# Transposing attention weights with the DMA crossbar instead of the matrix engine

## The chip, the cores and the metric

The kernel runs on one core of a Trainium2 chip. A core has five engines that run their own instruction queues in order: TensorE (PE, matrix multiplications, with a separate row for its weight loads, PEld), VectorE (DVE), ScalarE (ACT), GpSimd (POOL) and SyncE (SP), which here issues all DMAs. Engines meet only through semaphores. PE writes to PSUM, the others work mostly in SBUF, 128 partitions wide. The metric is the device time of one execution in microseconds, the median of the runs; lower is better.

## The reference

Attention that keeps the 32 largest scores of each row, and then a feed-forward block with a hard-swish gate.

```python
B, H, S, D = 8, 8, 576, 64          # float32 throughout
scores = (1 / sqrt(D)) * q @ k.T
kth    = 32nd largest of each row
scores = where(scores >= kth, scores, -1e9)
attn   = exp(scores - max) / (sum + 1e-9)
x      = (attn @ v)                 # (B,H,S,D) -> (B*S, H*D) = (4608, 512)
h      = x @ w_in                   # (512, 2048)
out    = (h * clip(h + 3, 0, 6) / 6) @ w_out   # (2048, 512)
```

## The kernel before

Work is cut into 80 *duos* (L184). A duo is two head pairs (a `Pair`, L138, is two heads of one batch element, put one above the other on the 128 partitions) and one tile of query rows. S = 576 is four tiles of 128 rows and a rest of 64; a full duo has two rows of 576 scores per partition and head pair (`nt = 2`), a duo of the rests has one (`nt = 1`), because both heads' 64 rows share the partitions. A batch element has ten duos, eight full ones and two of rests, in the order full, full, rest, full, full, full, full, rest, full, full.

The order of all instructions is written by hand (`tc.manual_schedule()`, L66) in the loop over steps `m` (L482). What a step issues on each engine stands in that engine's queue in just that order. In step `m`:

- DVE does the eight rounds `top(0)` to `top(7)` of duo `m` (L240): four for head pair u=0, four for u=1. A round finds the next 8 largest values of each row (MAX8, L247) and, but for the last round, strikes them out (MATCH_REPLACE8, L251).
- `prev.exp(1)` and, after `top(3)`, `u.exp(0)` (L256): POOL computes the negated threshold `kth` (L262) and `shift` (L263, L264) from the scan, ACT applies a very steep Prelu (L267) and Exp (L272), which also sums the row into `den`; POOL adds a small constant to it (L277).
- `duos[m+1].scores()` (L197): PE multiplies q and k for the next duo into `big`, the one five-bank PSUM tile, and ACT copies the scores to `sc` (L230, L233; three buffers).
- after `top(1)`, `prev.weights()` (L279): one reciprocal of `den` on DVE (L281) for both head pairs, then four scalings of a row each on POOL (L285).
- after `top(2)`, `prev.transpose()` (L289): 18 PE transposes of 128x128 blocks (12 for rests) from `sc` into `big` (L298), and one ACT copy of all of them to `eT` (L302).
- after `top(6)`, `values(m - 1)` (L418, L304): PE multiplies v by `eT` (L316), ACT copies the result into `xT`, the input of the feed-forward (L323). When a tile of 256 rows is complete, its feed-forward block is put into the list `todo`.
- `piece(n)` (L394) takes the next pieces of the feed-forward generator (L327) from that list: PE's `h` (L340), ACT's relu (L348), DVE's gate (L352, issued two pieces later), PE's `acc` (L361), ACT's scaling and SP's store of the output (L371, L373). How many pieces a step takes depends on the length of the list when the program is built. What is left after the last step follows at the end.

In the first steps every round also calls `convert_step`. The weights `w_in` and `w_out` come as 64-bit floats and are turned into 32-bit ones in 32 chunks (`convert`, L97): SP loads a chunk `st` (L103), ACT takes both halves of each word apart (L108, L111), POOL clamps (L109), and one or two conversion steps later DVE shifts and combines (L117, L118) and POOL adds (L122).

The loads of the next batch element's k and q (`load`, L145, six DMAs) and v (`load_values`, L159, four DMAs) are issued by SP after `top(0)` in the fourth to seventh step of a batch, one pair a step; its k and q are transposed by PE (L176) after `top(4)` of the sixth to ninth step. v lies in a ring of eight sets of tiles, `vm` and `vr`, and k's rests in `kr`. The pool `kq` has nine buffers of 4.6 KB per partition, which hold `landed`, the transposed `kq` and the chunks `st`. SP takes its DMAs strictly in the order of the program, and each waits there for what it needs.

Of the kernel before, what the change touches and what calls it, by code (L numbers as in the profile page):

```python
# [9 lines left out]
ALU = mybir.AluOpType  # L10
F32 = mybir.dt.float32
U32 = mybir.dt.uint32
I32 = mybir.dt.int32
PSUM = bass.MemoryType.PSUM

TOP_K = 32
# [11 lines left out]
def kernel(  # L28
# [22 lines left out]
    def pool(name, bufs, **kw):  # L51
        return ctx.enter_context(tc.tile_pool(name=name, bufs=bufs, **kw))

    consts = pool("consts", 1)
    kqpool = pool("kq", 2 * NHP + 1)
    scpool = pool("sc", 3)
    wkpool = pool("wk", 1)
    mpool = pool("m", 4)
    etpool = pool("et", 1)
    xtpool = pool("xt", 2)  # L60
    xrpool = pool("xr", 1)
    gpool = pool("g", 8)
# [14 lines left out]

    ring = []  # L80
    for i in range(2 * NHP):
        vm = const([P, 2, J, D], f"vm{i}")
        vr = const([P, 2, D], f"vr{i}")
        kr = const([P, 2, R], f"kr{i}")
        nc.gpsimd.memset(vr[:], 0.0)
        nc.gpsimd.memset(kr[:], 0.0)
        ring.append((vm, vr, kr))

    def big():

        return ps_big.tile([P, 5 * 512], F32, tag="big", name="big")
# [46 lines left out]
    class Pair:  # L138


        def __init__(self, b, hp):
            self.b, self.hp = b, hp
            self.vm, self.vr, self.kr = ring[(b * NHP + hp) % len(ring)]

        def load(self):  # L145
            h0 = 2 * self.hp
# [23 lines left out]
        def transpose(self):  # L170
            kq = kqpool.tile([P, JP + S], F32, tag="kq", name="kq")
            self.kT, self.qT = kq[:, 0:JP], kq[:, JP : JP + S]
            ps = big()
            for j in range(2 * J + 1):
                rows = self.landed[:, j, :, :].rearrange("p h d -> p (h d)")
                nc.tensor.transpose(ps[:, j * P : (j + 1) * P], rows, ident[:])  # L176
            c0 = 2 * JP
            nc.scalar.copy(kq[:, 0:c0], ps[:, 0:c0])
            nc.scalar.copy(kq[:, c0 : c0 + R], ps[:, c0 + R : c0 + 2 * R])
            for hh in range(2):  # L180
                d = slice(hh * D, (hh + 1) * D)
                nc.scalar.copy(self.kr[d, hh, :], ps[d, c0 : c0 + R])  # L182

    class Duo:  # L184
# [6 lines left out]
        def __init__(self, pairs, qt):  # L191
            self.pairs, self.qt = pairs, qt
            self.rest = qt == J
            self.nt = 1 if self.rest else 2
            self.nb = J + 2 if self.rest else 2 * J + 1

        def scores(self, us=(0, 1)):  # L197

# [41 lines left out]
        def top(self, u, r):  # L240

            if r == 0:
                self.m = mpool.tile([P, 2, TOP_K], F32, tag="m", name="m")
                self.wk = wkpool.tile([P, 2, S], F32, tag="wk", name="wk")
                self.cur = [self.row(u, t) for t in range(self.nt)]
            for t in range(self.nt):
                nc.vector.max(self.m[:, t, 8 * r : 8 * r + 8], self.cur[t])  # L247
# [28 lines left out]
            d = self.den[:, u, 0:nt]  # L276
            nc.gpsimd.tensor_scalar_add(d, d, EPS)  # L277

        def weights(self):  # L279
            d = self.den[:, :, 0 : self.nt]  # L280
            nc.vector.reciprocal(d, d)  # L281
            for u in range(2):
                for t in range(self.nt):
                    row = self.row(u, t)
                    nc.gpsimd.tensor_scalar(  # L285
                        row, row, self.den[:, u, t : t + 1], 1.0, ALU.mult, ALU.mult
                    )

        def transpose(self):  # L289

            starts = [c * P for c in range(J)]
            starts += [JP, S - P] if self.rest else [c * P for c in range(J, 2 * J + 1)]
            eT = self.eT = etpool.tile([P, 2 * (2 * J + 1), P], F32, tag="eT", name="eT")
            ps = big()
            n = 0
            for u in range(2):
                for c0 in starts:
                    nc.tensor.transpose(  # L298
                        ps[:, n * P : (n + 1) * P], self.sc[:, u, c0 : c0 + P], ident[:]
                    )  # L300
                    n += 1
            nc.scalar.copy(eT[:, 0:n, :].rearrange("p c q -> p (c q)"), ps[:, 0 : n * P])  # L302

        def values(self, dst):  # L304

            w = R if self.rest else P
            pv = ps_w.tile([P, 512], F32, tag="w", name="pv")
            for u in range(2):
                pr, eT = self.pairs[u], self.eT[:, u * self.nb : (u + 1) * self.nb, :]
                for c in range(J + 1):  # L310
                    for hh in range(2):
                        if self.rest:
                            rhs = eT[:, c if c < J else J + hh, hh * R : (hh + 1) * R]
                        else:
                            rhs = eT[:, c if hh == 0 or c == J else J + 1 + c, :]
                        nc.tensor.matmul(  # L316
                            pv[hh * D : (hh + 1) * D, u * w : (u + 1) * w],
                            pr.vm[:, hh, c, :] if c < J else pr.vr[:, hh, :],
                            rhs,
                            start=(c == 0),  # L320
                            stop=(c == J),
                        )
            nc.scalar.copy(dst, pv[:, 0 : 2 * w].rearrange("p (u q) -> p u q", u=2))  # L323
# [56 lines left out]
    duos = []  # L380
    for b in range(B):
        halves = [pairs[b][0:2], pairs[b][2:4]]
# [5 lines left out]
    per_batch = 2 * J + 2  # L388
    ND = len(duos)
# [4 lines left out]
    def piece(count=1):  # L394
        nonlocal left
        for _ in range(count):
            while todo:
                try:
                    gates.append(next(todo[0]))
                    left -= 1  # L400
                    break
                except StopIteration:
                    todo.pop(0)
            else:
                gates.append(None)
            if len(gates) > 2:
                gate = gates.pop(0)
                if gate:
                    gate()
# [69 lines left out]
    convert_step(2)  # L479
    first[3].load()  # L480

    for m in range(ND + 1):  # L482
        u = duos[m] if m < ND else None
        prev = duos[m - 1] if m else None


        level = (left >= 10) + (left >= 20)
        if u and u.rest:
            count = [(1, 0, 1, 0), (1, 0, 1, 1), (1, 1, 1, 1)][level]
        else:  # L490
            count = [(2, 1, 2, 1), (2, 2, 2, 1), (2, 2, 2, 2)][level]
        depth = 2 if m < 2 else 1

        def top(r):
            if u:
                u.top(r // 4, r % 4)
            convert_step(depth)

        if m:
            prev.exp(1)  # L500
        else:
            first[2].transpose()
            first[3].transpose()
        if m + 1 < ND:
            duos[m + 1].scores()
        top(0)
        piece(count[0])
        p = pair_at(m, 3)
        if p:
            p.load()  # L510
            p.load_values()
        if m == 0:
            first[0].load_values()
# [22 lines left out]
        if m:  # L536
            values(m - 1)
        top(7)
        if m == 2:
            piece(3)  # L540
    while todo:
        piece()
    piece(2)


# [1 line left out]
_INS = ["q", "k", "v", "moe_w_in", "moe_w_out"]  # L547
# [30 lines left out]
```

## Time and profile before

| | |
|---|---|
| median of 3 runs | 1737.13 us (1736.5 to 1737.71) |
| the profiled execution | 1738.36 us |
| its span, first to last instruction | 1736.6 us |
| mean granted TensorE clock | 0.967 |
| PE busy | 1607.3 us, 93% of the span |
| DVE busy | 1544.7 us, 89% |
| ACT busy | 947.1 us, 55% |
| POOL busy | 413.8 us, 24% |
| DMA queue of SP | 100,992 packets, 54.55 MB, 11.4% of 16 engines |

Busy time is the time in which an engine has an instruction in work; matrix multiplications are pipelined, so a busy PE is not PE at its peak. In the tables of groups a line names source line, engine, operation, output <- input and the count, then busy us and the mean ns of one, then the idle time of the engine just before them and what ended it. A DMA line names the transfer, how often it is issued, its size and the median us from issue to landing. "Rows" of PE are counted by the hardware: a 32-bit multiplication of the program shows as two, a transpose as one.

### The profile page before, as it was taken

What the parts mean: (1) busy time and instruction counts of PE and PEld (TensorE: products, weight loads), DVE (VectorE), ACT (ScalarE), POOL (GpSimd) and SP (SyncE); (2) the same over time, 40 slices, a digit from 0 to 9 for tenths busy, and PEclk for the clock granted to TensorE, in tenths of its full rate; (3) what the DMA queues carried; (4) which work ended last, traced back from release to release, by engine and by line L of the source; (5) the groups of instructions that cost most, each with busy time, mean ns of one, the idle gap of its engine ahead of it and who ended that gap; (6) DMA issues with size and microseconds to landing.
All of it is one profiled execution on the core that took longest, in us unless ns stands there. A gap on an engine that the chain in (4) does not pass through costs nothing.

```text
span 1736.6 us, 26566 instructions
## 1 busy us (share of the span) xinstructions
PE 1607.3 (93%) x9824; PEld 1111.1 (64%) x9824; DVE 1544.7 (89%) x3169; ACT 947.1 (55%) x1559; POOL 413.8 (24%) x1030
## 2 busy tenths in 40 slices
PE   5257788999999999999999999999999999999999
PEld 2154656667666675767577575857578575858575
DVE  3979999999999999999999989998999999999310
ACT  4665655565555655556556555656556555556210
POOL 2773212221222212221222212221222212221100
PEclk9568988999999999999999999999999999999999
DMA  6442110010010101110102000210012000000000
GB/s 181 143 154 56 25 31 18 13 42 1 13 45 24 34 1 37 38 34 1 30 13 60 13 1 7 68 28 8 7 27 68 7 7 7 7 7 7 7 13 12
DMA packets 101121, 56.23 MB, mean 32 GB/s; under 512 B 84097, under 2 KB 92289, under 8 KB 100993
## 3 DMA queue, kind: packets, MB, share of 16 engines
q1 hardware_dynamic: 100992, 54.55, 11.4%
q8 instruction: 77, 1.26, 0.3%
q14 instruction: 52, 0.42, 0.1%
HBM read 45.09 MB, written 9.44 MB: 31 GB/s over the span
## 4 chain that ended last, share of the span: by engine, by line
DVE 50%; PE 38%; ACT 5%; POOL 4%; issue 2%; SPq 0%; DMA 0%; ACTq 0%; POOLq 0%
DVE m L247 25%; DVE wk L251 20%; PE acc L361 16%; PE h L340 8%; PE pv L316 4%; PE big L298 4%; DVE g L352 3%; PE big L224 3%; POOL sc L285 2%; ACT sc L272 1%; PE big L176 1%; ACT eT L302 1%; PE big L227 1%; PE big L212 1%; DVE y L118 1%
## 5 line engine op out<-in xcount | busy, mean ns | idle before, releaser
L247 DVE MAX8 m<-wk 128x8 f32<-128x576 f32 x864 | 614.8, 749 | 2.3
L361 PE MATMUL acc<-w_out,g 128*128 128x512 f32 x1152 | 513.0, 594 | 0.0
L340 PE MATMUL h<-xT,w_in 128*128 128x256 f32 (+1 forms) x2304 | 462.6, 358 | 2.6 <-ACT xT L323 2.6
L340 PEld LDWEIGHTS h<-xT,w_in 128*128 128x128 f32 x2304 | 395.6, 192 | 49.1 <-issue 4.0
L251 DVE MATCH_REPLACE8 wk<-m,wk 128x576 f32<-128x576 f32 x576 | 424.4, 745 | 0.0
L361 PEld LDWEIGHTS acc<-w_out,g 128*128 128x128 f32 x1152 | 212.2, 191 | 230.0 <-issue 228.1
L302 ACT COPY eT<-big 128x2304 f32<-128x2304 f32 (+1 forms) x80 | 156.2, 1952 | 231.0 <-PE big L298 231.0
L298 PE MATMUL big<-ident,sc 128*128 128x128 f32 x1344 | 191.2, 292 | 88.4 <-POOL sc L285 84.7
L267 ACT ACTIVATE sc<-sc,kth 128x576 f32<-128x576 f32 x288 | 209.3, 770 | 109.3 <-POOL kth L262 109.2
L298 PEld LDWEIGHTS big<-ident,sc 128*128 128x128 f32 x1344 | 160.1, 149 | 137.1 <-POOL sc L285 126.7
L285 POOL TENSOR_SCALAR sc<-sc,den 128x576 f32<-128x576 f32 x288 | 212.8, 755 | 137.6 <-DVE den L281 134.7
L272 ACT ACTIVATE sc<-sc,shift 128x576 f32<-128x576 f32 x288 | 219.4, 763 | 3.1 <-POOL shift L264 0.2
L247 DVE MAX8 m<-sc 128x8 f32<-128x576 f32 x288 | 204.0, 746 | 15.2 <-ACT sc L233 15.2
L251 DVE MATCH_REPLACE8 wk<-m,sc 128x576 f32<-128x576 f32 x288 | 212.2, 744 | 0.0
L352 DVE SCALAR_TENSOR_TENSOR g<-g,h 128x512 f32<-128x512 f32 x144 | 97.3, 676 | 122.9 <-ACT g L348 122.8
L348 ACT ACTIVATE g<-h,three 128x512 f32<-128x512 f32 x144 | 98.0, 683 | 150.5 <-PE h L340 145.0
L316 PE MATMUL pv<-eT,vm 128*64 128x128 f32 (+1 forms) x2560 | 163.0, 272 | 9.3 <-ACT eT L302 8.7
L316 PEld LDWEIGHTS pv<-eT,vm 128*64 128x64 f32 x2560 | 135.8, 141 | 51.1 <-issue 24.7
L277 POOL TENSOR_SCALAR den<-den 128x2 f32<-128x2 f32 (+1 forms) x160 | 35.6, 223 | 545.3 <-ACT sc L272 545.3
L262 POOL TENSOR_SCALAR kth<-m 128x2 f32<-128x2 f32 (+1 forms) x160 | 36.0, 225 | 472.5 <-DVE m L247 471.4
L224 PE MATMUL big<-kq 64*128 64x512 f32 x512 | 131.6, 633 | 7.4 <-ACT kr L182 7.4
L230 ACT COPY sc<-big 128x2048 f32<-128x2048 f32 (+1 forms) x65 | 118.6, 1824 | 20.0 <-PE big L227 20.0
(46 smaller groups left out, 992.4 us busy)
## 6 DMA issues: line engine op xcount, KB each, us to landing
landed<-in_k_dram SPq DMA_DIRECT2D x64, 128.0 KB, 2.9
landed<-in_q_dram SPq DMA_DIRECT2D x64, 128.0 KB, 2.8
st<-in_moe_w_in_dram SPq DMA_DIRECT2D x16, 512.0 KB, 4.1
vm<-in_v_dram SPq DMA_DIRECT2D x64, 128.0 KB, 2.3
st<-in_moe_w_out_dram SPq DMA_DIRECT2D x16, 512.0 KB, 3.6
out_dram<-o SPq DMA_DIRECT2D x32, 256.0 KB, 2.3
landed<-in_k_dram SPq DMA_DIRECT2D x32, 32.0 KB, 2.5
landed<-in_q_dram SPq DMA_DIRECT2D x32, 32.0 KB, 2.5
```

Of the source, the lines that this page charges most:

```text
L224: nc.tensor.matmul(banks[:, 2 * i + hh, :], pr.qT[d, qs], pr.kT[d, :])
L247: nc.vector.max(self.m[:, t, 8 * r : 8 * r + 8], self.cur[t])
L251: nc.vector.match_replace(wk, self.m[:, t, 8 * r : 8 * r + 8], self.cur[t], LOWEST)
L267: nc.scalar.activation(row, row, AF.Prelu, bias=kth[:, t : t + 1], scale=1.0, alpha=STEEP)
L272: nc.scalar.activation(row, row, AF.Exp, bias=shift[:, t : t + 1], scale=scale, accum_out=self.den[:, u, t : t + 1],)
L285: nc.gpsimd.tensor_scalar(row, row, self.den[:, u, t : t + 1], 1.0, ALU.mult, ALU.mult)
L298: nc.tensor.transpose(ps[:, n * P : (n + 1) * P], self.sc[:, u, c0 : c0 + P], ident[:])
L302: nc.scalar.copy(eT[:, 0:n, :].rearrange("p c q -> p (c q)"), ps[:, 0 : n * P])
L316: nc.tensor.matmul(pv[hh * D : (hh + 1) * D, u * w : (u + 1) * w], pr.vm[:, hh, c, :] if c < J else pr.vr[:, hh, :], rhs, start=(c == 0), ...
L340: nc.tensor.matmul(h[:, (f - f0) * nt : (f - f0 + 1) * nt], w_in[:, i, f * P : (f + 1) * P], xT[:, i, 0:nt], start=(i == 0), stop=(i == NH ...
L352: nc.vector.scalar_tensor_tensor(out=g[:], in0=g[:], scalar=6.0, in1=h[:], op0=ALU.min, op1=ALU.mult)
L361: nc.tensor.matmul(acc[:], gs[f // nf][:, c0 : c0 + P], w_out[:, f, :], start=(f == 0), stop=(f == NFC - 1),)
```

## The change

The PE transposes of the weights and the ACT copy behind them are replaced. The crossbar of the DMA engines transposes 2-byte elements, and the weights are 4-byte floats. So for each head pair POOL copies a duo's scaled rows into a tile `e16` of 16-bit halves, all low halves first and then all high halves; SP issues one transposing DMA from `e16` to `t16` (18 blocks of 128x128 half-words, 12 for rests); and ACT, half a step later, joins the two planes to 32-bit words in `eT`.

What else moves with it:

- `weights` is done per head pair: for u=0 after `top(5)` of the duo's own step, for u=1 after `top(1)` of the next step. There are two reciprocals per duo in place of one.
- `join(0)` stands after `top(2)` and `join(1)` after `top(6)` of the next step.
- `values(m - 2)` stands after `top(1)`, in the place of `values(m - 1)` after `top(6)`; the loop has one step more, `ND + 2`, and the extra three pieces come at step 3 and not 2.
- `e16`, `t16` and `eT` are taken from the pool `kq`, which has 14 buffers in place of 9; the pool of `eT` is gone.
- v lies in four sets of tiles in place of eight, and is loaded in the second and third step of its own batch element, after the last use of the one before; k's and q's loads move one step later (`pair_at(m, 4)`).

The number of ordinary DMAs stays 392; 160 transposing ones are added, all on SP.

```diff
-    kqpool = pool("kq", 2 * NHP + 1)
+    kqpool = pool("kq", 14)
-    etpool = pool("et", 1)
...
-        def weights(self):
-            d = self.den[:, :, 0 : self.nt]
+        def weights(self, u):
+            d = self.den[:, u, 0 : self.nt]
             nc.vector.reciprocal(d, d)
...
+            n = self.nb * P
+            e16 = kqpool.tile([P, 2 * (2 * J + 1) * P], U16, tag="kq", name="e16")
+            halves = e16[:, 0 : 2 * n].rearrange("p (h x) -> p h x", h=2)
+            parts = [(0, S + R, 0), (S - P, S, S + R)] if self.rest else [(0, n, 0)]
+            for c0, c1, to in parts:
+                words = self.sc[:, u, c0:c1].bitcast(U16).rearrange("p (x h) -> p h x", h=2)
+                nc.gpsimd.tensor_copy(halves[:, :, to : to + c1 - c0], words)
+            t16 = kqpool.tile([P, 2 * (2 * J + 1), P], U16, tag="kq", name="t16")
+            self.t16[u] = t16
+            nc.sync.dma_start_transpose(t16[:, 0 : 2 * self.nb, :], e16[:, 0 : 2 * n])
-        def transpose(self):
...
-                    nc.tensor.transpose(
-                        ps[:, n * P : (n + 1) * P], self.sc[:, u, c0 : c0 + P], ident[:]
-                    )
...
-            nc.scalar.copy(eT[:, 0:n, :].rearrange("p c q -> p (c q)"), ps[:, 0 : n * P])
+        def join(self, u):
+            n = self.nb * P
+            eT = self.eT[u] = kqpool.tile([P, 2 * J + 1, P], F32, tag="kq", name="eT")
+            nc.scalar.copy(
+                eT[:, 0 : self.nb, :]
+                .rearrange("p c q -> p (c q)")
+                .bitcast(U16)
+                .rearrange("p (x h) -> p h x", h=2),
+                self.t16[u][:, 0 : 2 * self.nb, :].rearrange("p (h c) q -> p h (c q)", h=2),
+            )
...
-    for m in range(ND + 1):
+    for m in range(ND + 2):
...
-        p = pair_at(m, 3)
+        p = pair_at(m, 4)
         if p:
             p.load()
-            p.load_values()
...
         top(1)
-        if m:
-            prev.weights()
+        if prev:
+            prev.weights(1)
+        if m > 1:
+            values(m - 2)
+        if u and u.pairs[0].b and 1 <= m % per_batch <= 2:
+            for p in duos[m - 1].pairs:
+                p.load_values()
         piece(count[1])
         top(2)
-        if m:
-            prev.transpose()
+        if prev:
+            prev.join(0)
...
         top(5)
+        if u:
+            u.weights(0)
         piece(count[3])
         top(6)
-        if m:
-            values(m - 1)
+        if prev:
+            prev.join(1)
         top(7)
```

More of the change, by code (lines that the diff above doesn't have):

```diff
@@ L13 @@
 I32 = mybir.dt.int32
+U16 = mybir.dt.uint16
 PSUM = bass.MemoryType.PSUM
@@ L76 @@
     w_out = const([P, NFC, DM], "w_out")
[L80 to L87, printed above, removed]
+    vms = [const([P, 2, J, D], f"vm{i}") for i in range(NHP)]
+    vrs = [const([P, 2, D], f"vr{i}") for i in range(NHP)]
+    krs = [const([P, 2, R], f"kr{i}") for i in range(2 * NHP)]
+    for t in krs + vrs:
+        nc.gpsimd.memset(t[:], 0.0)
     def big():
@@ L142, in __init__ @@
             self.b, self.hp = b, hp
-            self.vm, self.vr, self.kr = ring[(b * NHP + hp) % len(ring)]
+            self.vm, self.vr, self.kr = vms[hp], vrs[hp], krs[b % 2 * NHP + hp]
         def load(self):
@@ L195, in __init__ @@
             self.nb = J + 2 if self.rest else 2 * J + 1
+            self.t16, self.eT = [None] * 2, [None] * 2
         def scores(self, us=(0, 1)):
@@ L277, in exp @@
             nc.gpsimd.tensor_scalar_add(d, d, EPS)
-        def weights(self):
-            d = self.den[:, :, 0 : self.nt]
+        def weights(self, u):
+            d = self.den[:, u, 0 : self.nt]
             nc.vector.reciprocal(d, d)
[L282 to L286, printed above, removed]
-                    )
@@ L289, in transpose @@
-        def transpose(self):
[L291 to L298, printed above, removed]
-                        ps[:, n * P : (n + 1) * P], self.sc[:, u, c0 : c0 + P], ident[:]
-                    )
-                    n += 1
-            nc.scalar.copy(eT[:, 0:n, :].rearrange("p c q -> p (c q)"), ps[:, 0 : n * P])
+            for t in range(self.nt):
+                row = self.row(u, t)
+                nc.gpsimd.tensor_scalar(
+                    row, row, self.den[:, u, t : t + 1], 1.0, ALU.mult, ALU.mult
+                )
@@ new lines, in weights @@
+            self.t16[u] = t16
[9 more added lines that the diff above has]
+                self.t16[u][:, 0 : 2 * self.nb, :].rearrange("p (h c) q -> p h (c q)", h=2),
+            )
@@ L308, in values @@
             for u in range(2):
-                pr, eT = self.pairs[u], self.eT[:, u * self.nb : (u + 1) * self.nb, :]
+                pr, eT = self.pairs[u], self.eT[u]
                 for c in range(J + 1):
@@ L480 @@
     first[3].load()
-    for m in range(ND + 1):
+    for m in range(ND + 2):
         u = duos[m] if m < ND else None
-        prev = duos[m - 1] if m else None
+        prev = duos[m - 1] if 0 < m <= ND else None
         level = (left >= 10) + (left >= 20)
@@ L497, in top @@
             convert_step(depth)
-        if m:
+        if prev:
             prev.exp(1)
-        else:
+        elif m == 0:
             first[2].transpose()
@@ L533 @@
         top(5)
+        if u:
+            u.weights(0)
         piece(count[3])
         top(6)
-        if m:
-            values(m - 1)
+        if prev:
+            prev.join(1)
         top(7)
-        if m == 2:
+        if m == 3:
             piece(3)
```

## The prediction

> **What bounds the kernel now.** I read the windows by stage first, then who waited for whom, then the groups, then the timelines of one early step and of the end. The columns of the first are: stretch, its length, busy us and instructions of PE, weight loads, DVE, ACT and POOL, granted PE clock, DMA share, GB/s.
>
> ```profile
> 57.00:87.00 30.00, 11.36 (x70) 8.57 (x70) 30.00 (x58) 18.21 (x32) 22.32 (x29) 0.61 0.45 143
> ...
> 151.00:170.00 19.00, 12.69 (x76) 8.68 (x78) 19.00 (x41) 10.87 (x17) 4.40 (x12) 0.74 0.08 23
> 170.00:1623.00 1453.00, 1408.77 (x8734) 974.68 (x8732) 1401.92 (x2904) 838.36 (x1377) 320.96 (x885) 0.99 0.08 22
> 1623.00:1737.00 114.00, 109.70 (x592) 74.23 (x588) 8.44 (x13) 16.92 (x26) 3.71 (x8) 1.00 0.04 12
> ```
>
> Three stages. Up to about 170 us the weights are converted between the scans: DVE is full, PE is not. From 170 to 1623 PE is busy 97% and DVE 96.5%: two engines bound it almost equally. The last 114 us are PE alone. Where DVE still waits in the middle stage (columns: waiter, releaser, us in total, times, longest):
>
> ```profile
> DVE g L352 <- ACT g L348: 35.2, 18, 4.2
> DVE den L281 <- POOL den L277: 10.4, 16, 1.6
> ```
>
> So behind PE (g comes from PE's h) DVE loses only 35.2 us there. That is the purse a lighter PE can pay from, although the transposes keep PE busy five times as long:
>
> ```profile
> L298 PE MATMUL big<-ident,sc 128*128 128x128 f32 x1344 | 191.2, 292 | 88.4 <-POOL sc L285 84.7
> L302 ACT COPY eT<-big 128x2304 f32<-128x2304 f32 x64 | 133.2, 2081 | 207.2 <-PE big L298 207.2
> L285 POOL TENSOR_SCALAR sc<-sc,den 128x576 f32<-128x576 f32 x288 | 212.8, 755 | 137.6 <-DVE den L281 134.7
> L277 POOL TENSOR_SCALAR den<-den 128x2 f32<-128x2 f32 (+1 forms) x160 | 35.6, 223 | 545.3 <-ACT sc L272 545.3
> landed<-in_k_dram SPq DMA_DIRECT2D x64, 128.0 KB, 2.9
> st<-in_moe_w_in_dram SPq DMA_DIRECT2D x16, 512.0 KB, 4.1
> vr<-in_v_dram SPq DMA_DIRECT2D x64, 16.0 KB, 2.1
> ```
>
> **Prices of what the trace does not show.** Split (2304 half-words on POOL): 576 elements cost 755 ns, 2 cost 223, so 0.93 ns an element and 0.22 + 2304 x 0.93 = 2.4 us. Ends: 1.3 us, if half-words run at half that price; 5.5 us at the two-input rate of L122 (1362 ns for 512 elements, the 2-element L263 197 ns: 2.3 ns each). I take 2.4, the one-input row. Join (2304 half-words on ACT): L302 moves 2304 elements in 2.08 us; ends 1.0 (by bytes) and 3.1 (the 770 ns per 576 of L267); I take 2.1. Crossing (576 KB by DMA): the floor is vr's 2.1 us. Above it, landed's 256-byte runs cost 0.8 us for 112 KB more, so 4.1 us for 576 KB; st's 4 KB runs 2.0 for 496 KB, so 2.3. The blocks are 16 rows of 128 half-words, 256 bytes a row, nearest to landed: 6.2 us to land, ends 4.4 and, for a crossing that writes pieces a quarter as long at landed's price per run, 2.1 + 16.4 = 18.5.
>
> The Trainium skill speaks against the change: "VectorE: DVE Perf Modes", The three transpose paths, gives the crossbar 1309 ns for one 128x128 block of 2-byte elements and TensorE 390; L298's row has 292 ns for the latter. Eighteen blocks in turn would be an estimated 23.6 us, two of them 47 us in a step, and the whole kernel 64 x 47 + 16 x 31, some 3,500 us. "DMA: Bandwidth & Descriptors", Latency and other measured facts, gives 261 GB/s instead: an estimated 2.3 us of transfer, and by it the sum below falls by some 10 us. No row here can decide between them.
>
> **The change, part by part.** *PE* loses L298 and ACT loses L302 (156.2 us with its short form). In the middle stage PE falls by about 174 us to 85% of it. At 67% busy (151 to 170 us) the granted clock was 0.74, so some clock may go; at 0.86 PE's 1235 us would be 1436, still inside 1453. *ACT* gains 128 x 2.1 + 32 x 1.4 = 314 us and ends near 64% busy: no bound. *POOL* gains about 128 x 2.4 + 32 x 1.8 = 365 us, to 45%. *DVE* gains 80 reciprocals; back to back one takes 0.1 us of its queue: +8 us, on the path, since DVE is now the bound.
>
> *Middle stage, the chain that must fit.* After the sixth round of a step (u=0) or its second (u=1): scale 1.5, split 2.4, crossing 6.2, join 2.1, which is 12.2 us. The join stands in ACT's queue ahead of the next exp of that half (kth, shift 0.65; Prelu and Exp 3.4; den 0.25), and DVE's next reciprocal waits for that: 16.7 us with the reciprocal, against a median full step of 21. Covered. A step of leftover rows is 12.8 us. The sixth round of the step before ended 4.5 us before it begins, so scale, split and crossing land at 5.6 us of it, join at 7.7, one-row exp and den 9.7, and DVE comes to the reciprocal at 9 to 10: just covered. Each further us of crossing would cost twice 15 us. I take the den waits as 25 us (twice as many places) against 10.4, the g waits as 16 against 35.2 (ACT, busier, still delays some), and 8 for the reciprocals: **+4**, rounded with the clock to +8. Ends: -38 (both waits gone, 8 paid) and, with the slowest crossing, the second rival.
>
> *Early stage.* This is the large term. SP issues in order, and SP now holds a transpose that waits for the split, with the next three or four weight loads (st) queued behind it; behind these on ACT stand L108 and L111, and behind them the next exp. What this stage has to spare:
>
> ```profile
> 67.13 4.62 POOL L285 TENSOR_SCALAR sc<-sc,den 128x576 f32<-128x576 f32 x4
> ```
>
> Little: POOL is busy 22.3 of 30 us there, and its four scalings took 4.62 us beside DVE's integer work against 4 x 0.73 later. From a reciprocal: scale 1.5 + split 2.4 + issue 0.6 + the crossing's 4.1 of transfer ahead on the queue + 4.1 for a load to land + 1.3 for the one behind it + 0.7 (L108) + 0.7 (L109) = 15.3 us until POOL is free for kth; kth, exp and den add 4.3: 19.6. DVE reaches the next reciprocal after four round places (2.77 + 1.33 + 2.77 + 2.77) and four conversions at 1.1, 14.0. It waits 5.6 us. Six half steps have such loads: four full ones 22 us; two in the leftover step, where DVE needs only 10, 19; and POOL, with 4.8 us more per step in a queue that is three quarters full, I put at 5 more: **+46 us**. Ends: +23 (crossing 4.4 and split 1.3 take 2.9 from each of the six, and POOL 5) and +120 (crossing 18.5 adds 12.3 to each).
>
> *Moved loads.* k and q loads go from the fourth to the fifth step of a batch, still one step before their transposes; v loads into four buffers, not eight, at the second and third step, one step before use. 12 DMAs at 0.6 us issue and under 3 us to land against 21: nothing; without the cover a PE wait, and PE has 2 us a step to spare. Outputs may leave some us later behind a transpose; only the last one counts, and no transpose is near it.
>
> *End.* Two rows of DVE's timeline, then two of PE's:
>
> ```profile
> 1621.58 1.42 DVE L247 MAX8 m<-wk 128x8 f32<-128x576 f32 x2
> 1626.92 0.18 DVE L281 RECIPROCAL den<-den 128x4 f32<-128x4 f32 x1 [3.93 <-POOL den L277]
> 1639.15 1.09 PE L316 MATMUL pv<-eT,vm 128*64 128x128 f32 x16
> 1648.45 14.45 PE L340 MATMUL h<-xT,w_in 128*128 128x128 f32 x128
> ```
>
> Now PE, 16.1 us after the last scan (1623.0), comes to the last values; 8 multiplications by w_out (16 rows of the trace, 7.0 us), 84.1 us of blocks and 4 us of stores follow.
>
> After the change: reciprocal 4.1, scale 1.5, split 2.4, crossing 6.2, join 2.1: values at 16.3 us, as now. But the program's order leaves 20 multiplications instead of 8 behind them, 12 x 0.86 = **+10 us**. Shortened by no lighter PE: the order is fixed.
>
> **Sum.** 1736.6 (the span) + 46 + 8 + 10 = 1800.6, and 1.8 lies around the span (1738.36 in that run, 0.07% above the median 1737.13): **1802 us**, 3.7% slower.
>
> **Rivals.** *Faster (10%)*: the 35.2 us of waits on g go, and the early loads hide because the split costs 1.3 and the crossing 4.4 us. 1737 - 35 + 8 + 10 = 1720 with an early stage that costs nothing, 1710 with no den waits either. For it: PE is at 97%. Against it: DVE at 96.5% leaves little to win, and SP's order holds the loads back whatever PE does. *Crossing or split paces the loop (24%)*: above 6.2 us each us costs 30 in the leftover steps, above 10.5 (21 less the chain's other 10.5) it costs 64 more in the full ones. The early stage adds 6 for each. At 8.5 us that is 1802 + 69 + 14 = 1885; at 12.5, 1802 + 189 + 128 + 38 = 2157. A longer split lengthens the same chains, and kth stands behind it on POOL: 5.5 us is 3.1 more at the same 30 + 6, 1914. For it: no row prices a crossing. Against it: DMA is only 8% busy in the middle. *Nothing measurable (3%)*: early loss and middle gain cancel, 1737; it needs the early +46 halved and the whole purse.
>
> **How the numbers follow.** The stated course has 63%, 1760 to 1850 by its bounds; likeliest 1802. The range goes down to 1750, leaving most of the faster case out, and up to 1950, a crossing near 10.3 us (1802 + 123 + 25 = 1950): about 2 in 10 lie outside. A measurement of this kernel tells 0.2%, 3.5 us, from no change. Faster 10%, same 3%, slower 87%.
>
> **What would show it.** Right: scans of the sixth duo starting near 216 us instead of 170, DVE waiting on L281's successor and the conversions' first DVE operation before then; st loads issued right after a transpose; the middle near 1460 us with DVE over 95% and PE near 85%; an end of about 124. Wrong: transposes landing over 9 us after issue, ACT waiting on DMA before the join in every step; or an early stage no longer than 185 us.

## The result, and the profile after

The changed kernel takes 1792.76 us (median of 4 runs, 1789.43 to 1793.89) against 1737.42 for the kernel before on the same chip: a ratio of 1.0316, interval 1.0298 to 1.0334. The forecast was 1802 us. The profiled span is 1791.7 us, 55.1 more than before, and the mean granted clock of TensorE falls from 0.967 to 0.923.

Cut at the sixth duo's first scan and at the end of the last scan, as in the prediction (us):

| stage | before | after | difference | predicted |
|---|---|---|---|---|
| early, weights being converted | 170.1 | 220.4 | +50.3 | +46 |
| middle | 1452.9 | 1448.3 | -4.6 | +8 |
| end, after the last scan | 113.6 | 123.0 | +9.4 | +10 |

The two cuts come from DVE's timeline of the kernel after:

```profile
220.40 1.40 DVE L245 MAX8 m<-sc 128x8 f32<-128x576 f32 x2
...
1667.34 1.41 DVE L245 MAX8 m<-wk 128x8 f32<-128x576 f32 x2
```

The windows of the kernel after (stretch, its length, busy us and instructions of PE, weight loads, DVE, ACT and POOL, granted PE clock, DMA share, GB/s):

```profile
59.00:108.00 49.00, 7.34 (x32) 4.11 (x32) 35.66 (x60) 18.97 (x31) 26.84 (x32) 0.50 0.39 111
108.00:155.00 47.00, 9.20 (x52) 5.71 (x52) 25.25 (x41) 21.30 (x30) 26.47 (x31) 0.54 0.38 114
...
221.00:1669.00 1448.00, 1303.88 (x7464) 856.39 (x7458) 1404.10 (x2976) 1066.71 (x1452) 621.94 (x1064) 0.96 0.40 80
1669.00:1792.00 123.00, 118.07 (x600) 78.27 (x600) 10.12 (x16) 21.55 (x29) 4.21 (x7) 0.99 0.09 21
```

DVE, which was busy without a gap from 57 to 87 us before, is busy 36 of 49 and then 25 of 47 us: in these two stretches no engine is full any more, so something waits in turn. In the middle PE has fallen by 105 us to 90% and DVE stays at 97%: one engine bounds it where two did, and the length hardly moves.

What the new operations cost, by the groups and the DMA issues of the kernel after:

```profile
L296 POOL COPY e<-sc 128x2304 uint16<-128x2304 uint16 x128 | 269.4, 2105 | 8.1
L305 ACT COPY eT<-t 128x2304 uint16<-128x2304 uint16 x128 | 357.2, 2790 | 38.8 <-DMA t<-e 38.5
L284 DVE RECIPROCAL den<-den 128x2 f32<-128x2 f32 x128 | 19.7, 154 | 25.3 <-POOL den L275 25.2
t<-e SPq DMA_TRANSPOSE x160, 4.6
st<-in_moe_w_in_dram SPq DMA_DIRECT2D x16, 512.0 KB, 5.2
```

The split takes 2.1 us, the join 2.8, and a crossing lands 4.6 us after its issue. Who DVE waited for, first up to 220 us:

```profile
DVE a L114 <- POOL a L106: 43.9, 10, 10.8
DVE m L245 <- ACT sc L231: 15.6, 1, 15.6
DVE den L284 <- POOL den L275: 13.3, 5, 5.2
```

and then from 221 to 1669 us:

```profile
DVE den L284 <- POOL den L275: 25.7, 30, 3.9
DVE g L361 <- ACT g L357: 13.0, 11, 2.6
```

The early stage can be added up from DVE alone. Before, its waits on POOL's clamp (L109 there, L106 now) were 16.7 us and there were none of note on `den`: +27.2 and +13.3. Its two conversion operations took 48.7 us before and take 59.0 now (32.4 in L115, 26.6 in L114): +10.3. Together that is 50.8; a wait of 2.6 us on a gate, which the kernel before had there, falls away, and DVE's other work grows by 1.4: 49.6 of the 50.3 measured. The middle likewise: waits on `g` -22.2, on `den` +15.3, busy time +2.2, together -4.7 against -4.6.

One early half step in the timeline (start, length, instruction, idle time before it and its releaser) shows the order of events:

```profile
80.23 2.22 POOL L296 COPY e<-sc 128x2304 uint16<-128x2304 uint16 x1
80.40 2.58 DVE L115 SCALAR_TENSOR_TENSOR y<-st,y 128x512 uint32<-128x512 uint32 x1
...
82.47 2.67 SPq L299 DMA_TRANSPOSE t<-e  x1
...
85.23 1.48 SPq L100 DMA_DIRECT2D st<-in_moe_w_in_dram  x3
...
86.02 0.68 DVE L115 SCALAR_TENSOR_TENSOR y<-st,y 128x512 uint32<-128x512 uint32 x1
...
90.13 0.66 ACT L105 ACTIVATE a<-st 128x512 f32<-128x512 f32 x1 [13.01 <-DMA st<-in_moe_w_in_dram]
...
95.29 0.23 POOL L260 TENSOR_SCALAR kth<-m 128x2 f32<-128x2 f32 x1
...
98.60 0.22 POOL L275 TENSOR_SCALAR den<-den 128x2 f32<-128x2 f32 x1 [2.61 <-ACT sc L270]
98.85 0.17 DVE L284 RECIPROCAL den<-den 128x2 f32<-128x2 f32 x1 [5.24 <-POOL den L275]
```

The transpose issues 0.02 us after the split has ended (80.23 + 2.22), the loads directly after the transpose. ACT has then stood 13 us for the first of them, and 8.7 us after that the next reciprocal still comes 5.24 us late. The same lines hold a second effect: L115 takes 2.58 us beside the split, and 0.68 in the same step without it.

### The profile page after: what moved, and what is told of

The parts are those of the page before. It is cut to its first block, busy times and chain, and to the rows that moved or that the text cites. A ratio compares the mean times of both kernels' runs of the same rounds, so it can differ in the third digit from the quotient of the medians.

```text
span 1791.7 us, 24696 instructions
## 1 busy us (share of the span) xinstructions
PE 1502.2 (84%) x8480; PEld 986.7 (55%) x8480; DVE 1560.9 (87%) x3249; ACT 1190.7 (66%) x1639; POOL 735.2 (41%) x1218
## 2 busy tenths in 40 slices
DMA packets 450302, 144.23 MB, mean 80 GB/s; under 512 B 433280, under 2 KB 441472, under 8 KB 450176
## 4 chain that ended last, share of the span: by engine, by line
DVE 64%; PE 14%; ACT 12%; POOL 3%; issue 3%; DMA 3%; SPq 0%; ACTq 0%; POOLq 0%
DVE m L245 32%; DVE wk L249 26%; PE acc L370 7%; DVE g L361 4%; PE h L349 4%; ACT eT L305 3%; ACT sc L270 3%; ACT sc L228 2%; PE big L222 2%; ACT sc L265 2%; PE pv L325 1%; DMA st<-in_moe_w_out_dram 1%; DMA t<-e 1%; DMA st<-in_moe_w_in_dram 1%; POOL a L106 1%
## 5 line engine op out<-in xcount | busy, mean ns | idle before, releaser
L370 PE MATMUL acc<-w_out,g 128*128 128x512 f32 x1152 | 523.4, 602 | 6.2 <-DVE g L361 6.2
L349 PE MATMUL h<-xT,w_in 128*128 128x256 f32 (+1 forms) x2304 | 474.8, 364 | 33.6 <-DVE g L361 22.2
L349 PEld LDWEIGHTS h<-xT,w_in 128*128 128x128 f32 x2304 | 402.6, 195 | 90.9 <-issue 19.1
L305 ACT COPY eT<-t 128x2304 uint16<-128x2304 uint16 (+1 forms) x160 | 418.4, 2615 | 39.6 <-DMA t<-e 39.3
L296 POOL COPY e<-sc 128x2304 uint16<-128x2304 uint16 (+1 forms) x192 | 321.2, 1683 | 10.1
L325 PE MATMUL pv<-eT,vm 128*64 128x128 f32 (+1 forms) x2560 | 182.2, 285 | 127.2 <-ACT eT L305 87.6
L325 PEld LDWEIGHTS pv<-eT,vm 128*64 128x64 f32 x2560 | 148.1, 148 | 178.0 <-ACT eT L305 93.0
L222 PE MATMUL big<-kq 64*128 64x512 f32 x512 | 144.0, 685 | 73.9 <-ACT kr L179 34.6
L222 PEld LDWEIGHTS big<-kq 64*128 64x128 f32 x512 | 48.6, 206 | 142.0 <-issue 46.4
L228 ACT COPY sc<-big 128x2048 f32<-128x2048 f32 (+1 forms) x65 | 118.4, 1822 | 11.2 <-PE big L225 10.9
```

Of the source, the lines that this page charges most:

```text
L222: nc.tensor.matmul(banks[:, 2 * i + hh, :], pr.qT[d, qs], pr.kT[d, :])
L296: nc.gpsimd.tensor_copy(halves[:, :, to : to + c1 - c0], words)
L305: nc.scalar.copy(eT[:, 0 : self.nb, :] .rearrange("p c q -> p (c q)") .bitcast(U16) .rearrange("p (x h) -> p h x", h=2), self.t16[u][:, 0 ...
L325: nc.tensor.matmul(pv[hh * D : (hh + 1) * D, u * w : (u + 1) * w], pr.vm[:, hh, c, :] if c < J else pr.vr[:, hh, :], rhs, start=(c == 0), ...
L349: nc.tensor.matmul(h[:, (f - f0) * nt : (f - f0 + 1) * nt], w_in[:, i, f * P : (f + 1) * P], xT[:, i, 0:nt], start=(i == 0), stop=(i == NH ...
L370: nc.tensor.matmul(acc[:], gs[f // nf][:, c0 : c0 + P], w_out[:, f, :], start=(f == 0), stop=(f == NFC - 1),)
```

## The experiments

All were timed in several rounds beside the kernel before; in the order of the table that kernel's median was 1736.50 us for the first four, 1737.41 for the next three and 1737.45 for the last two. Stages as above:

| run | early | middle | end | median | ratio to before, interval |
|---|---|---|---|---|---|
| loads ahead | 179.6 | 1446.2 | 123.0 | 1751.24 | 1.0086 (1.0071 to 1.0101) |
| first duos by PE | 167.1 | 1442.8 | 123.0 | 1736.36 | 0.9998 (0.9989 to 1.0008) |
| move alone | 167.5 | 1506.2 | 124.3 | 1799.79 | 1.0363 (1.0347 to 1.0378) |
| cross twice | 220.9 | 1570.8 | 130.5 | 1919.22 | 1.1056 (1.1040 to 1.1073) |
| split twice | 220.5 | 1520.8 | 125.2 | 1867.50 | 1.0747 (1.0732 to 1.0761) |
| pieces on before | 169.0 | 1477.8 | 92.7 | 1741.77 | 1.0026 (1.0016 to 1.0036) |
| first by PE, pieces | 169.6 | 1440.8 | 90.2 | 1701.45 | 0.9795 (0.9781 to 0.9808) |
| first by PE, split kept | 179.6 | 1444.6 | 123.0 | 1747.53 | 1.0057 (1.0043 to 1.0071) |
| more pieces late | 169.2 | 1450.0 | 80.4 | 1699.44 | 0.9781 (0.9767 to 0.9795) |

**Loads ahead.** The changed kernel, but the weight chunks are loaded up to four conversions ahead, so that they stand in SP's queue in front of the transpose.

```diff
-    def convert(dst, src):
+    def load_chunk(dst, src):
+        st = kqpool.tile([P, 2 * WC], U32, tag="kq", name="st")
+        nc.sync.dma_start(st[:], src)
+        return dst, st
+    def convert(dst, st):
...
+    loaded = []
+    def load_ahead(n):
+        while chunks and len(loaded) < n:
+            loaded.append(load_chunk(*chunks.pop(0)))
...
-        if chunks:
-            c = convert(*chunks.pop(0))
+        if loaded:
+            c = convert(*loaded.pop(0))
...
+        if ahead[0]:
+            load_ahead(4)
```

> The changed kernel with the weight loads st issued four chunks earlier in the program, so that they stand on SP ahead of the transpose that waits for the split; nothing else moves. Theory (SP's order holds the loads back): the scans of the sixth duo start at 160 to 175 us instead of 220, ACT no longer waits 80 us for st, the middle and the end stay (1448 and 123), total about 1743. Rival (POOL's split and its clash with DVE's integer work fill the early stage): the sixth duo still starts after 200 us, total 1772 or more.

Measured: 1751.24 us. The early stage falls from 220.4 to 179.6 us, a little less far than expected; the others stay within 2.1. DVE's waits of this run up to 165 us:

```profile
DVE a L117 <- POOL a L109: 18.4, 5, 11.1
...
DVE den L287 <- POOL den L278: 0.7, 2, 0.4
```

The waits are almost those of the kernel before (16.7 and none). The same instructions, transposes and loads ran; only their order in one queue changed, and 40.8 of the 50.3 us came back. That the loads stood behind the waiting transpose is thereby shown. 9.5 us stay. Issuing the transposes from another engine's queue was not tried.

**First duos by PE.** The first four duos of the changed kernel are transposed by PE again, at the place of the join and for one head pair at a time; their splits and transposing DMAs fall away.

```diff
+            if self.m_at < 4:
+                return
             n = self.nb * P
             e16 = kqpool.tile([P, 2 * (2 * J + 1) * P], U16, tag="kq", name="e16")
...
+            if self.m_at < 4:
+                starts = [c * P for c in range(J)]
+                starts += [JP, S - P] if self.rest else [c * P for c in range(J, 2 * J + 1)]
+                ps = big()
+                for i, c0 in enumerate(starts):
+                    nc.tensor.transpose(
+                        ps[:, i * P : (i + 1) * P], self.sc[:, u, c0 : c0 + P], ident[:]
+                    )
+                nc.scalar.copy(eT[:, 0 : self.nb, :].rearrange("p c q -> p (c q)"), ps[:, 0:n])
+                return
...
+    for i, duo in enumerate(duos):
+        duo.m_at = i
```

> The first four duos keep the changed order (halves, joins, values a step later) but are transposed by PE and copied from PSUM by ACT, with no split and no crossing; all later duos as in the changed kernel. Both theories expect the early stage back: sixth duo at 158 to 172 us, total about 1738 to 1745. What lies between this run and the one with the loads issued ahead is the share of POOL's split in the early loss: 0 to 8 us by the theory of SP's order, 30 or more by the rival. If the early stage stays over 200 us here, the loss comes from the moved order itself and not from the crossing.

Measured: 1736.36 us, no difference from the kernel before. The early stage is 167.1 us, shorter even than the 170.1 of before: the whole loss of that stage sits in the first duos' splits and crossings. It is also 12.5 us better than loading ahead, more than the 0 to 8 that the theory gave the split, so something besides the queue costs there. A window of this run's middle:

```profile
167.00:1610.00 1443.00, 1295.97 (x7481) 850.03 (x7481) 1404.58 (x2977) 1067.21 (x1452) 622.31 (x1066) 0.96 0.40 81
```

The four kernels whose middle is the same (the changed one, this one, loads ahead and the next) have it at 1442.8 to 1448.3 us. The change thus saves 5 to 10 us of the middle's 1452.9, and the longer end takes 9.4 back.

**First duos by PE, split kept.** The kernel just shown, but the first four duos' splits run all the same; nothing reads them.

```diff
-            if self.m_at < 4:
-                return
             n = self.nb * P
...
                 nc.gpsimd.tensor_copy(halves[:, :, to : to + c1 - c0], words)
+            if self.m_at < 4:
+                return
             t16 = kqpool.tile([P, 2 * (2 * J + 1), P], U16, tag="kq", name="t16")
```

> As the run whose first four duos are transposed by PE, but POOL makes the split of those four duos all the same; its result is not used and nothing crosses. It prices POOL's share of the early loss alone. With the loads ahead of the transpose the sixth duo came at 179.6 us, without split and crossing at 167.1. Theory (the 12.5 us left over are POOL's queue and its clash with DVE's integer work): sixth duo at 174 to 181, total 1742 to 1749. Rival (they are the crossing: its transfer beside the weight loads and its place on SP): sixth duo below 171, total within 4 us of 1736.

Measured: 1747.53 us, 11.2 more than without the splits, and the same early 179.6 us as with loads ahead. DVE's waits of this run up to 165 us, and below them those of the run without the splits:

```profile
DVE a L114 <- POOL a L106: 18.4, 5, 11.1
```

```profile
DVE a L114 <- POOL a L106: 14.0, 4, 11.1
```

That is 4.4 us more; L115 takes 34.7 us against 30.0 and L114 22.7 against 21.0, 6.4 more. So the splits' own cost, some 11 us, is shown: a little of it is POOL's queue, the larger part DVE's integer work running slower beside them. With loads ahead, where splits and crossings both ran, the stage took the same 179.6 us, so nothing is left there for the crossing itself: of the 220.4 us, 12.5 are the splits and 40.8 the order in SP's queue.

**Move alone.** All duos are transposed by PE, in the new order and half by half: the moved scalings, values and loads without the crossbar (`80` in place of `4` in both conditions).

```diff
-            if self.m_at < 4:
+            if self.m_at < 80:
```

> All duos in the changed order, but all transposed by PE, each half into the one PSUM tile big and copied from there by ACT: the move without the crossing. Theory: early stage as before (sixth duo at 158 to 172 us), the middle PE-bound again and no better than before (1453), up to 60 us worse because big is now claimed three times a step, the end 10 us longer than before; total 1750 to 1810, DVE waiting on g for over 30 us. Rival (values a step later and the smaller waits are what helps the middle): middle at or below 1448.

Measured: 1799.79 us; early stage and end as in the run with four duos by PE, the middle 63.4 us longer. Its window and two of its waits there:

```profile
168.00:1674.00 1506.00, 1397.94 (x8741) 966.14 (x8740) 1408.03 (x2976) 850.79 (x1452) 323.32 (x886) 0.99 0.08 22
```

```profile
DVE den L284 <- POOL den L275: 63.7, 43, 3.9
...
PE big L222 <- ACT eT L315: 67.0, 58, 2.6
```

`big`, the one tile of PSUM that scores and transposes share, is now claimed three times a step, and PE's scores wait 67 us for ACT's copies out of it, which they never did in this stage of the kernel before. DVE's waits on `den` and `g` grow by 59 us against the run with four duos by PE. So the new order by itself is a loss in the middle, and the crossbar, which needs no `big`, is what pays for it. For transposes on PE the order of before, with one claim for both head pairs, is the better one.

**Cross twice.** From the fifth duo on, every transposing DMA is issued twice (`m_at` is the duo's number, as above).

```diff
-            nc.sync.dma_start_transpose(t16[:, 0 : 2 * self.nb, :], e16[:, 0 : 2 * n])
+            for _ in range(2 if self.m_at >= 4 else 1):
+                nc.sync.dma_start_transpose(t16[:, 0 : 2 * self.nb, :], e16[:, 0 : 2 * n])
```

> From the fifth duo on every crossing is issued twice into the same tile, the second after the first has landed: the join's data come 4.6 us later (9.2 in place of 4.6), early stage and values unchanged. By the prediction's price (30 us for each us in the leftover steps once scale, split, crossing and join pass 12.2 us; they are 11.0 now): 15.6, so 3.4 us beyond and about +100 in the middle, with DVE's waits on den at 100 or more and ACT waiting for t; total 1880 to 1900. Rival (the crossing lies hidden in a step of 21 us, leftover steps do not matter): less than +20.

Measured: 1919.22 us, the middle 122.5 us longer where about 100 was expected. ACT's wait before the join and DVE's before the reciprocal, over the middle:

```profile
ACT eT L306 <- DMA t<-e: 375.2, 116, 7.6
```

```profile
DVE den L284 <- POOL den L275: 134.5, 57, 7.1
```

A late crossing stops ACT at the join, then the exp behind it, then the reciprocal: the predicted chain. The price is 122.5 / 4.6 = 27 us for each us. But it isn't all paid where the prediction said: a leftover step grows from 13.0 to 17.4 us, 66 us over the 15 of this stage, and a full step from 20.9 to 21.8, 56 over 60. Of these 56, 30 lie in just eight steps, those directly behind a batch element's second leftover step.

**Split twice.** From the fifth duo on, POOL copies each split twice.

```diff
-                nc.gpsimd.tensor_copy(halves[:, :, to : to + c1 - c0], words)
+                for _ in range(2 if self.m_at >= 4 else 1):
+                    nc.gpsimd.tensor_copy(halves[:, :, to : to + c1 - c0], words)
```

> From the fifth duo on POOL makes every split twice into the same tile: 2.1 us more on POOL per half before the crossing (1.3 in the leftover duos), nothing else changed. The run with every crossing twice lost 122 us in the middle for 4.6 us, of which 58 in the full steps, where the prediction had none. Theory (split and crossing are one chain to the join): no more than 2.1/4.6 of that, +25 to +55 in the middle. Rival (kth of the next exp stands behind the split on POOL, a second path that the crossing does not touch): more per us than the crossing, +65 to +95, with the next exp on ACT waiting for kth.

Measured: 1867.50 us, the middle 72.5 us longer for 2.1 us more of split: 35 us for each us, dearer than the crossing's 27, as the rival had it. The timeline of a step of this run:

```profile
939.84 4.27 POOL L297 COPY e<-sc 128x2304 uint16<-128x2304 uint16 x2
944.08 0.22 POOL L260 TENSOR_SCALAR kth<-m 128x2 f32<-128x2 f32 x1
...
944.33 1.44 ACT L265 ACTIVATE sc<-sc,kth 128x576 f32<-128x576 f32 x2 [2.51 <-POOL kth L260]
```

`kth`, a fifth of a microsecond of work, starts the moment the two copies have ended, and ACT's Prelu has waited 2.51 us for it. In full duos `kth` starts on average 0.8 us (u=0) and 1.5 us (u=1) after the last scan round, against 0.09 in the changed kernel; in leftover duos 3.5 and 1.9, against 1.4 and 0.2. DVE's waits over the middle of this run:

```profile
DVE den L284 <- POOL den L275: 74.2, 35, 2.7
DVE g L362 <- ACT g L358: 34.1, 28, 4.5
```

Of the 74.2 us, 67.8 are 30 waits in the 15 leftover steps, and before each of them the Prelu had waited for `kth`; with the crossing twice none had, it was the join there. So the split delays two chains: its own crossing, and the threshold behind it on POOL, and in the leftover steps the second one is what DVE waits for. The full steps' share, 26 us, is mostly gates: the waits on `g` are 34.1 us where they were 13.0.

**Pieces on before.** PE has become lighter, and the order takes no use of it: how many feed-forward pieces a step takes is fixed when the program is built. Here the kernel before takes them as early as it can.

```diff
-        level = (left >= 10) + (left >= 20)
+        level = 2 + (m >= ND - 2)
...
-            count = [(1, 0, 1, 0), (1, 0, 1, 1), (1, 1, 1, 1)][level]
+            count = [0, 0, (2, 1, 2, 1), (2, 2, 2, 2)][level]
...
-            count = [(2, 1, 2, 1), (2, 2, 2, 1), (2, 2, 2, 2)][level]
+            count = [0, 0, (2, 2, 2, 2), (3, 2, 3, 2)][level]
```

> The kernel before with a freer rule for the feed-forward pieces (always 2 a place, 6 in leftover steps, 10 and 8 in the last two steps), so that less is left for the end; transposes by PE. Theory: PE is full in the middle, so what the end saves (113.6 to about 92) the middle pays: total within 10 us of 1737, DVE's waits on g well over 35 us. Rival (the list of pieces was simply badly set): 15 us or more faster.

Measured: 1741.77 us, slightly slower than before. The end is 20.9 us shorter and the middle 24.9 longer. Window and DVE wait of the middle:

```profile
170.00:1647.00 1477.00, 1423.48 (x8760) 985.90 (x8761) 1400.92 (x2902) 840.23 (x1379) 321.96 (x883) 0.99 0.08 22
```

```profile
DVE g L352 <- ACT g L348: 64.4, 38, 3.8
```

PE was full there already; DVE's gates wait 64.4 us for it where they waited 35.2.

**First duos by PE, and pieces.** The same three lines on top of the kernel with four duos by PE.

```diff
-        level = (left >= 10) + (left >= 20)
+        level = 2 + (m >= ND - 2)
...
+            count = [0, 0, (2, 1, 2, 1), (2, 2, 2, 2)][level]
...
+            count = [0, 0, (2, 2, 2, 2), (3, 2, 3, 2)][level]
```

> The run whose first four duos are transposed by PE, with the same freer rule for the pieces. Theory: the crossing left PE about 10% idle in the middle, so pieces taken earlier cost DVE little there: end 123 to about 90, middle at or below 1443, total 1685 to 1710, faster than both kernels. Rival (pieces in a step delay scores and gates, so that DVE waits): middle longer by what the end saves, total 1725 or more.

Measured: 1701.45 us, ratio 0.9795 (0.9781 to 0.9808): 2% faster than the kernel before, and so faster than both. Its window of the middle and the wait on `g` there:

```profile
168.00:1608.00 1440.00, 1318.18 (x7528) 862.60 (x7527) 1406.09 (x2977) 1064.83 (x1454) 624.01 (x1066) 0.95 0.40 81
```

```profile
DVE g L373 <- ACT g L369: 9.9, 19, 1.2
```

The end is 32.8 us shorter than in the kernel it was made from and the middle is not longer: PE does 22 us more in the middle and DVE isn't kept waiting. What the transposes had occupied on PE is worth 35 us, once the order puts other work there.

**More pieces late.** The last kernel with one step more at the higher count, and twelve pieces in such a step.

```diff
-        level = 2 + (m >= ND - 2)
+        level = 2 + (m >= ND - 3)
...
-            count = [0, 0, (2, 2, 2, 2), (3, 2, 3, 2)][level]
+            count = [0, 0, (2, 2, 2, 2), (3, 3, 3, 3)][level]
```

> The fastest run so far (first four duos by PE, freer pieces) with 12 pieces instead of 10 and 8 in the last three steps instead of two: the end some 9 us shorter (90 to about 81), the middle longer by 5 to 12 as the scans of those steps wait for gates; total 1695 to 1706, no clear change.

Measured: 1699.44 us, and the two intervals overlap: no clear difference. 9.8 us left the end and 9.2 came into the middle. PE has no room left in the last steps, as the stretch before the last scan's end shows:

```profile
1557.00:1619.00 62.00, 62.00 (x360) 42.56 (x357) 52.62 (x110) 36.59 (x51) 23.24 (x39) 1.00 0.28 57
```

## Why the prediction was right, and where its steps were off

**Early stage, +46 against +50.3: the mechanism is shown, and one term was small.** The prediction put 41 us on SP's order (22 in full half steps, 19 in the leftover step); loading ahead gave 40.8 back. It put 5 us on POOL; the split kept without its crossing costs 11.2 in the total and 12.5 in this stage. The moved order, which the sum left out, gives some 3 back (167.1 against 170.1). The POOL term counted POOL's queue, not that DVE's integer work slows down beside POOL's; the kernel before shows that already, with the same operation at 0.68 us in one place and at 1.75 beside POOL's add of the conversions:

```profile
68.20 0.68 DVE L118 SCALAR_TENSOR_TENSOR y<-st,y 128x512 uint32<-128x512 uint32 x1
...
84.89 1.43 POOL L122 TENSOR_TENSOR w_in<-a,y 128x512 int32<-128x512 int32 x1
...
85.12 1.75 DVE L118 SCALAR_TENSOR_TENSOR y<-st,y 128x512 uint32<-128x512 uint32 x1
```

The prices inside the 41 were further off than their sum: the crossing landed in 4.6 us and not 6.2, the split took 2.1 and not 2.4, but the transpose held SP's queue for 2.67 us and not the assumed 0.6, and the loads behind it landed in 5.2 us and not 4.1. (The eight terms add up to 15.4 us and not 15.3, which changes nothing.) And DVE did not wait mostly at the reciprocal, where the working stood, but at the first operation of the conversions (27.2 us of the increase against 13.3), which the list of signs had named.

**Middle, +8 against -4.6: the waits were right, a small term was not.** The prediction took 25 us of waits on `den` and 16 on `g`; the trace has 25.7 and 13.0. It added 8 us for 80 reciprocals and rounded the clock up by 4. The reciprocals did grow, from 12.7 to 23.1 us in this stage, yet DVE's busy time grew by 2.2 only: its 2,700 operations of the scans (MAX8, MATCH_REPLACE8 and the load of the values before it) are each 4 to 5 ns shorter than before, 9.6 us together, and two gates fewer, 2.0 us, fall into the stage. Neighbouring instructions overlap a little in these rows, so they don't add up to the 2.2 exactly. Why the scans are shorter wasn't tried and stays open.

**PE did not fall as far as said.** The prediction had 174 us less, to 85%; it was 105, to 90%. The groups of this stage show where the rest went: the 174.7 us of transposes did go, but the granted clock fell from 0.99 to 0.96 and the rows that stay grew, `h` (xT) from 372 to 379 ns, `acc` from 595 to 604, `pv` (vm) from 269 to 282 and the scores of full duos from 618 to 657. Growth of 2 to 6% isn't the clock's 3% alone; what else lengthens these rows stays open. With DVE at 97% and 13.0 us of waits on `g` left, that could cost little. That a lighter PE couldn't shorten the middle by more than the purse of 35.2 us was right; 22.2 of them came. The moved loads, put at nothing, made PE wait 16.2 us for v; a PE at 90% could bear it:

```profile
PE pv L325 <- DMA vm<-in_v_dram: 16.2, 19, 1.9
```

**End, +10 against +9.4: right.** PE has 20 multiplications of `acc` instead of 8 behind the last values. It is an order written into the program, no price of the crossbar: taking pieces earlier made that end 90.2 us, shorter than before the change.

**The rivals.** "Faster" needed early loads that hide and a middle 35 us shorter. The first four duos by PE give the former, and the gain was still only 10 in the middle less 9 at the end: nothing measurable. "Crossing or split paces the loop" didn't happen at 4.6 and 2.1 us, but doubling each shows how near it was.

There the working fell short: "above 6.2 us each us costs 30 in the leftover steps, above 10.5 (21 less the chain's other 10.5) it costs 64 more in the full ones". At 9.2 us, below that second point, 56 of the 122.5 us fell in full steps. Thirty of them are still the leftover steps' price: in the eight full steps behind a batch element's second leftover step, DVE waits 28.8 us at the first reciprocal, and that is the leftover duo's own. The chain begins in a short step and ends in the next one, where the working had no price. With the leftover steps' 66 that makes 96, near the 102 that the prediction's 30 us for each us gives: scale 1.5, split 2.1 and join 2.8 leave 5.8 of the covered 12.2 to the crossing, and 9.2 is 3.4 more. The other 26 are spread over 52 full steps, half a microsecond each, with gates and without; the working had nothing there, and their cause stays open. Its yardstick for full steps was also too long: 21 us is their mean in the kernel before (21.1), the median is 20.5, and steps without gates last 19.3.

For the split the prediction gave the same price as for the crossing and did name `kth` behind it; measured is 35 us per us against 27, because that second chain costs as well, and in the leftover steps of that run it is the one that DVE waits for.

**The crossbar's price.** Of the two rules of the Trainium skill weighed in the prediction, the trace decides. "VectorE: DVE Perf Modes", The three transpose paths, would have made 18 blocks in turn an estimated 23.6 us; they land in 4.6, so the 1309 ns of one block don't add up. "DMA: Bandwidth & Descriptors", Latency and other measured facts, comes near: 4.6 us less the 2.1 of a small load is 2.5 us for 576 KB, an estimated 236 GB/s against the stated 261.

## What to carry to other kernels

A DMA that waits for a computed value holds everything behind it in an in-order queue: look first at what stands there, because moving those loads ahead of it recovered 40.8 of 50.3 us here with the same work done. Time freed on one of two balanced engines is worth little (5 to 10 us of 1,453 here) until a fixed order puts other work into it, and the same reordering that loses on the full engine (+4 us before) can win on the relieved one (-35 us after). Hold a chain that must fit into a loop against the shortest steps, follow it into the step in which it ends, and ask what else queues behind each of its links.

## What the runs showed of the hardware that was not expected

- A transposing DMA occupies the issuing queue: 2.67 us for 18 blocks of 128x128 half-words, against 0.36 us for an ordinary load in the same step and 1.48 for three of them.
- These 16-bit copies, which write (ACT) or read (POOL) every second half-word, are not cheaper by their bytes: 2,304 half-words take ACT 2.79 us and POOL 2.1, while the 2,304 32-bit words of the replaced copy out of PSUM took ACT 2.08.
- DVE's combining step (L115, two 32-bit inputs) takes 2.58 us beside POOL's half-word copy and 0.68 in the same step without it. The scans' MAX8 shows no such effect: 744 ns on average with 735 us of POOL work in the span, 749 before with 414.
- The transposes bring many small packets: 450,302 in the span against 101,121, all of the added ones under 512 bytes (433,280 against 84,097), and the DMA share of the middle rises from 0.08 to 0.40. The chunks of `w_out` land in 5.2 us (median), where they took 3.6 before and 3.3 with the first duos by PE; how much of that is the transposes beside them and how much the bursts they come in was not separated.
